# Third to seventh batch on the second batch's schedule of folds and transforms, in an attention and Fourier-mixing kernel on one core

## The chip, the core and the metric

The kernel runs on one core of a Trainium2 chip. The core has five engines that take their instructions from queues of their own: TensorE (PE in the profile, with PEld for its weight loads), VectorE (DVE), ScalarE (ACT), GpSimd (POOL) and SyncE (SP), which here issues the DMA transfers. The metric is the device time of one execution in microseconds (us); lower is better.

## What is computed

Eight batches of 576 tokens, 8 heads of 64 channels. The first half is attention in which each query keeps its 32 largest scores; the second half is a Fourier mix over tokens and channels followed by an MLP of width 2048. Cut from the reference:

```python
scores = scale * np.matmul(q, k.transpose(0, 1, 3, 2))
kth = np.partition(scores, -32, axis=-1)[..., -32:-31]
scores = np.where(scores >= kth, scores, -1e9)
attn = softmax(scores)                      # max subtracted, divided by the sum
x = heads_to_channels(np.matmul(attn, v))   # (8, 576, 512)
X = np.fft.fft(np.fft.fft(x, axis=1), axis=2)
u = x + np.real(X)
un = (u - mean(u)) / np.sqrt(var(u) + 1e-6)
out = u + np.maximum(un @ w_ch1, 0.0) @ w_ch2
```

## The kernel before

**Tiles and steps.** A tile is 128 query rows of one head. A pair of heads makes nine tiles, a batch 36, the whole 288. The main loop runs one step `i` for each tile. In step `i` DVE finds the last of tile `i`'s 32 largest scores and the first of tile `i+1`'s (MAX8 at L422, MATCH_REPLACE8 at L424: four and three of each per tile); PE makes the scores of tile `i+3` (L398, the tails of the keys L368; the fifth tile of a pair, which holds the last rows of both heads and has `e` None, L383); ACT copies them to SBUF (L401, L372, L390). `bounds(i)` on POOL (`nt`, L431) turns the maxima into two biases; in the next step ACT makes the mask (L445), POOL subtracts it (L448) and ACT takes the exponential (L456). From the second batch on (except the last pair of the second batch and of the eighth) ACT splits the result into halves of words (L469), SP writes them to DRAM and reads them back transposed (L482, L485, L503), and PE multiplies by `v` in `attend` (L561) once a chunk of a pair is there.

**After a batch's attention.** `end` is the batch's last tile. The tokens' transform uses symmetry: `fold_tails` and `fold_ops` add and subtract halves of the tokens and the channels. `fold_ops(b, par, eng)` gives four operations for one parity of the output tokens: `sd` (L716), `zw` (L675), then `both` (the first eight instructions into `fg`) and the last (`third(2)`: four more). Their buffers have two tags in turn: `sd` and `fg` share "fold_s", `zw` has "fold_d", so the second parity's `sd` can be written only once PE has read the first parity's `fg`. `dft_tokens(b, par)` is the matmul with `fg` (`yp`, L752) and ACT's copies into `y`. `dft_channels(b, t)` (`mp`, L809 and L813) makes the channels' transform of token tile `t`, `add_mixed` adds it to `x` on POOL (L836), `stats` takes mean and variance on DVE, and `channels_first` (`tpu`, L878) transposes the sum for the MLP.

**The MLP in units.** `mlp_units(b)` cuts a batch's MLP into about 67 units: `hidden` (`hp`, L963, four matmuls) and `back` (`cp`, L990, two matmuls with 512 columns; L1029 for the tails). The first chunk of every batch but the first one uses a seven-product form instead (`cv`, `cw`, `cz`, L1160) with weight pieces brought back by DMA (L906) and sums on POOL (L1105, L1132). An fp32 matmul has two records in the profile. The units are appended to one queue when a batch arrives.

**What sets the order.** Everything is written out at build time. `at(step, where, fn, cost)` puts an operation into a plan; each step runs the plan's places in a fixed order. On PE the order is: scores, transposes of inputs, `pe1` (token transforms), `pe2` (channel transforms), `pe` (`channels_first`), the tails of the scores; `attend` follows at the end of a step. On POOL: the subtraction of the mask for tile `i-1`, then `pool0` (the folds), then `bounds(i)`, then `pool` and `pool2`. Between PE's fixed operations `some(limit)` takes units from the queue until a step's planned length `step_us` is reached. At each arrival `level` picks that length so that the queue is empty at the next arrival, by the planner's own costs (1.75 for a `back` unit, 8 x columns / 1200 for a `hidden` one):

```python
steps = range(i, next((a for a in arrivals if a > i), i + PER_BATCH))
rest, lev = sum(u[0] for u in queue + waiting), 0.0
while lev < 6.4 and sum(max(0.0, lev - fixed_cost(s)) for s in steps) < rest:
    lev += 0.02
```

What is over at the last arrival, and the last batch's own units, is worked off after the last tile.

**The schedule of a batch.** `T0` is `end` + 2 for the first batch, + 3 for the second (`soon`), + 4 for the last and + 5 for the others. `ft` holds the steps of the two token transforms, `fc` the first of the three steps of the channel transforms; the arrival is `fc` + 4 for all batches but the first and the last. The lines that the change touches stand at the end of this loop (L1375 to L1430).

Of the kernel before, what the change touches and what calls it, by code (L numbers as in the profile page):

```python
# [73 lines left out]
def kernel(  # L74
# [9 lines left out]
    nc = tc.nc  # L84
# [560 lines left out]
    def fold_channels(eng, z, f, c, n):  # L645

        def tt(dst, out, src, up, down, op):
            eng.tensor_tensor(out=dst[..., out], in0=src[..., up], in1=src[..., down], op=op)

        if n == 0:  # L650
            eng.tensor_copy(out=c[..., 0:Q1 + 1:Q1], in_=z[..., 0:Q1 + 1:Q1])
            up, down = slice(1, Q1), slice(Q2 - 1, Q1, -1)
            tt(c, up, z, up, down, ALU.add)
            tt(c, slice(Q1 + 1, Q2), z, up, down, ALU.subtract)
        elif n == 1:
            up, down = slice(0, Q0), slice(Q1, Q0, -1)
            tt(f, slice(0, Q0), c, up, down, ALU.add)
            tt(f, slice(Q1, Q1 + Q0), c, up, down, ALU.subtract)
            up, down = slice(Q1 + 1, Q1 + Q0), slice(Q2 - 1, Q1 + Q0, -1)
            tt(f, slice(Q0 + 1, Q1), c, up, down, ALU.subtract)  # L660
            tt(f, slice(Q1 + Q0 + 1, Q2), c, up, down, ALU.add)
            eng.memset(f[..., Q0:Q0 + 1], 0.0)
            eng.tensor_copy(
                out=f[..., Q1 + Q0:Q1 + Q0 + 1], in_=c[..., Q1 + Q0:Q1 + Q0 + 1]
            )
        else:
            up, down = slice(Q2 + 1, Q3), slice(DM - 1, Q3, -1)
            tt(f, up, z, up, down, ALU.subtract)
            tt(f, slice(Q3, DM - 1), z, up, down, ALU.add)
            eng.tensor_copy(out=f[..., Q2:Q2 + 1], in_=z[..., Q2:Q2 + 1])  # L670
            eng.tensor_copy(out=f[..., DM - 1:DM], in_=z[..., Q3:Q3 + 1])

    def fold_halves(eng, s_, z):
        for cols, op in ((slice(0, Q2), ALU.add), (slice(Q2, DM), ALU.subtract)):
            eng.tensor_tensor(out=z[..., cols], in0=s_[..., 0:Q2], in1=s_[..., Q2:DM], op=op)  # L675

    def fold_tails(b, eng):


        f, got = ftail[0:TAIL], []  # L680

        def first():
            got.append(batp.tile([P, DM + Q2], F32, name=f"zt_{b}", tag="fold_s")[0:TAIL])
            fold_halves(eng, x_of[b][0:TAIL, 4, :], got[0][:, 0:DM])
            channels(0)

        def channels(n):
            fold_channels(eng, got[0][:, 0:DM], f[:, 0:DM], got[0][:, DM:DM + Q2], n)

        def second():  # L690
            channels(1)
            eng.tensor_copy(out=f[:, DM:DM + 1], in_=got[0][:, DM + Q0:DM + Q0 + 1])

        return [first, second, lambda: channels(2)]

    def fold_ops(b, par, eng, space="own"):

        x = x_of[b]  # L700

        if space == "hT":
            sp = batp.tile([P, NIT * CW[0]], F32, name=f"fsp_{b}", tag="hT")

        def buf(n, name, cols=DM):
            if space == "hT":
                return sp[:, 2 * DM * n:2 * DM * n + 2 * cols].rearrange("p (s c) -> p s c", s=2)
            pool, tag = (batp, ("fold_s", "fold_d")) if space == "own" else (attp, ("PT0", "PT1"))
            return pool.tile([P, 2, cols], F32, name=f"{name}_{b}_{par}", tag=tag[n % 2], bufs=1)

        got = folded[b, par] = []

        def first():
            got.append(buf(0, "sd"))
            op = ALU.add if par == 0 else ALU.subtract
            eng.tensor_tensor(out=got[0], in0=x[:, 0:2, :], in1=x[:, 2:4, :], op=op)  # L716

        def second():
            got.append(buf(1, "zw"))
            fold_halves(eng, got[0], got[1])  # L720

        def third(n):
            if n == 0:
                got.append(buf(2, "fg", DM + Q2))
            fold_channels(eng, got[1], got[2][:, :, 0:DM], got[2][:, :, DM:DM + Q2], n)

        def both():
            third(0)
            third(1)

        return [first, second, both, lambda: third(2)]

    def dft_tokens(b, par):
        for g2 in range(2):
            half_of_tokens(b, par, g2)
        return 4.3
# [96 lines left out]
    def add_mixed(b, t):  # L833
        rows, x = ROWS[t], x_of[b]
        us = us_of[b, t > 1 and t < 4][0:rows, CHUNKS[CHUNK_OF[t][0]].index(t), :]
        nc.gpsimd.tensor_tensor(out=x[0:rows, t, :], in0=x[0:rows, t, :], in1=us, op=ALU.add)  # L836

    def stats(b, t):
        rows, mvb = ROWS[t], mv[b % 2]
        st6 = small.tile([P, 6], F32, name=f"st6_{b}_{t}", tag="st6")  # L840
        nc.vector.bn_stats(out=st6[0:rows], in_=x_of[b][0:rows, t, :])
        nc.vector.bn_aggr(out=mvb[0:rows, t, :], in_=st6[0:rows])
# [454 lines left out]
    def at(step, where, fn, cost=0.0):  # L1297
        plan.setdefault((step, where), []).append(fn)
        costs[step] = costs.get(step, 0.0) + cost
# [75 lines left out]
    for b in range(B):  # L1375
        end = PER_BATCH * (b + 1) - 1
        last = b == B - 1
        first, soon = b == 0, b == 1
        T0 = end + (2 if first else 3 if soon else 4 if last else 5)
        if first:  # L1380

            for op in fold_tails(b, nc.gpsimd):
                at(T0 - 1, "pool", op)

            def folds(b=b):
                for par, space in ((0, "own"), (1, "hT")):
                    for op in fold_ops(b, par, nc.vector, space):
                        op()
            at(T0, "dve", folds)
            ft, fc = (T0 + 1, T0 + 1), T0 + 1  # L1390
        elif soon:

            for n, op in enumerate(fold_tails(b, nc.gpsimd)):
                at(T0 - 2 + n, "pool0", op)
            for par in range(2):
                def folds(par=par, b=b, T0=T0):
                    for n, op in enumerate(fold_ops(b, par, nc.gpsimd)):
                        at(T0 + 1 + 3 * par + min(n, 2), "pool0", op)
                at(T0, "begin", folds)
            ft, fc = (T0 + 4, T0 + 7), T0 + 8  # L1400
        elif not last:
            for n, op in enumerate(fold_tails(b, nc.gpsimd)):
                at(T0 - 2 + n, "pool0", op)
            for par in range(2):
                def folds(par=par, b=b, T0=T0):
                    for n, op in enumerate(fold_ops(b, par, nc.gpsimd)):
                        at(T0 + (6 if par else 1) + n, "pool0", op)
                at(T0, "begin", folds)
            ft, fc = (T0 + 5, T0 + 11), T0 + 12
        else:  # L1410
            for op in fold_tails(b, nc.gpsimd):
                at(T0 - 1, "pool0", op)

            def folds(b=b):
                for op in fold_ops(b, 0, nc.vector) + fold_ops(b, 1, nc.vector, "PT"):
                    op()
            at(T0, "dve", folds)

            at(T0 + 1, "pe1", lambda: one_unit() + one_unit() if len(queue) > 1 else 0.0)
            ft, fc = (T0 + 1, T0 + 3), T0 + 4  # L1420
        for par in range(2):
            at(ft[par], "pe1", lambda b=b, par=par: dft_tokens(b, par), 4.3)
        for n, t in enumerate((0, 1, 4, 2, 3)):
            quick = first or last
            s = fc + (0 if first else n // 3 if last else n // 2)
            at(s, "pe2", lambda b=b, t=t, q=quick: dft_channels(b, t, q), 1.75)
            if not quick:
                at(s, "pool2", lambda b=b, t=t: add_mixed(b, t))
                at(s + 1, "dve", lambda b=b, t=t: stats(b, t))
            at(s + (1 if quick else 2), "pe", lambda b=b, t=t: channels_first(b, t), 0.6)  # L1430
            if first and t == 4:
                at(s + 1, "pe", lambda: (queue.extend(waiting), waiting.clear()) and 0.0)
        at(s + 1, "begin" if quick else "dve", lambda b=b: rsqrt(b))
        arrivals.append(s + (1 if quick else 2))
        at(arrivals[-1], "units", lambda b=b: (queue if b else waiting).extend(mlp_units(b)))
# [36 lines left out]
    def one_unit():  # L1472
        c, fn, _ = queue.pop(0)
        fn()
        return c
# [175 lines left out]
```

## Time and profile before

| what | us |
|---|---|
| median of 3 runs (1879.72 to 1884.17) | 1882.73 |
| the profiled execution, own time | 1882.96 |
| its span, first to last instruction | 1881.2 |
| PE busy / DVE busy / ACT busy / POOL busy | 1713.1 / 1582.7 / 1295.7 / 911.3 |
| MAX8 on scores still being worked on (L422, 864 of them) | 626.5, 749 ns each |
| `sd` of a fold on POOL (L716, 12 of them) | 28.4, 2368 ns each |
| PE waiting at `sp_t` (L368) for ACT's copies L390, 16 times | 24.4 |

The page cuts the span into 40 slices of 47 us and gives each engine's busy share in tenths. A PE record's length is modelled, so PE can be busy in the view and still have room. A wait is put down to whoever released it. The tiles' top-k ends at 1684.5 us of the span; what follows is PE work of the last batch, with the seventh batch's left-over units ahead of it.

### The profile page before, as it was taken

How to read it: one execution, taken by the hardware profiler on the slowest of the kernel's cores; microseconds unless marked ns; L12 is line 12 of the kernel's file. 1: busy time of each engine (PE TensorE's matmuls, PEld its weight loads, DVE VectorE, ACT ScalarE, POOL GpSimd, SP SyncE). 2: the span in 40 equal slices, each digit the busy share in tenths (PEclk: the TensorE clock that was granted, in tenths of full speed). 3: DMA queues.
4: the chain of work that ended last, by engine and by line, in shares of the span. 5: the costliest groups of instructions: out<-in, count | busy, mean ns of one | idle time of the engine just before them, and what ended most of it. 6: DMA issues, size and time to landing. Idle time of an engine off the chain costs nothing.

```text
span 1881.2 us, 26922 instructions
## 1 busy us (share of the span) xinstructions
PE 1713.1 (91%) x8134; PEld 1086.5 (58%) x8134; DVE 1582.7 (84%) x3301; ACT 1295.7 (69%) x3104; POOL 911.3 (48%) x1278
## 2 busy tenths in 40 slices
PE   5567699889899998989999999999999999999999
PEld 3344364364466654666456665666556655666677
DVE  7999999798899999998899998999999999862110
ACT  6878658576788778777777677777787678652100
POOL 4768643455645356354544465355544465341012
PEclk8887899899899999999999999999999999999999
DMA  5333026651468755585455854685466756440132
GB/s 167 105 96 109 24 60 171 175 138 51 118 155 212 178 125 129 149 214 131 123 144 151 215 128 121 141 229 147 125 155 180 179 133 143 121 117 6 51 110 72
DMA packets 516576, 249.16 MB, mean 132 GB/s; under 512 B 398288, under 2 KB 506448, under 8 KB 516432
## 3 DMA queue, kind: packets, MB, share of 16 engines
q1 hardware_dynamic: 515664, 247.23, 50.7%
q8 instruction: 65, 1.06, 0.2%
q14 instruction: 79, 0.65, 0.1%
q10 hardware_dynamic: 768, 0.21, 0.0%
HBM read 93.63 MB, written 84.74 MB: 95 GB/s over the span
## 4 chain that ended last, share of the span: by engine, by line
PE 66%; ACT 10%; DVE 9%; POOL 7%; issue 3%; DMA 3%; SPq 2%; POOLq 0%; DVEq 0%; ACTq 0%
PE hp L963 24%; PE cp L990 8%; PE o L561 7%; PE sp L398 5%; DVE m L422 4%; PE cw L1160 4%; DVE wk L424 4%; PE yp L752 3%; PE cv L1160 3%; PE cp L1029 3%; POOL wk L448 2%; ACT wk L469 2%; ACT wk L445 2%; PE sp_t L368 2%; ACT S L456 1%
## 5 line engine op out<-in xcount | busy, mean ns | idle before, releaser
L448 POOL TENSOR_TENSOR wk<-S,wk 128x576 f32<-128x576 f32 x288 | 406.7, 1412 | 532.5 <-ACT wk L445 509.8
L422 DVE MAX8 m<-wk 128x8 f32<-128x576 f32 x864 | 626.5, 749 | 6.1
L963 PE MATMUL hp<-unT,w 128*128 128x256 f32 (+1 forms) x2048 | 535.3, 412 | 3.8 <-ACT hT L967 2.6
L963 PEld LDWEIGHTS hp<-unT,w 128*128 128x128 f32 x2048 | 379.4, 192 | 134.5 <-issue 33.4
L424 DVE MATCH_REPLACE8 wk<-m,wk 128x576 f32<-128x576 f32 x576 | 427.4, 742 | 0.0
L469 ACT COPY wk<-S 128x576 uint16<-128x576 uint16 x468 | 288.7, 666 | 0.0
L445 ACT ACTIVATE wk<-S,nt 128x576 f32<-128x576 f32 x288 | 222.5, 773 | 92.6 <-POOL nt L431 91.8
L422 DVE MAX8 m<-S 128x8 f32<-128x576 f32 x288 | 213.9, 743 | 45.1 <-ACT S L372 45.1
L990 PE MATMUL cp<-w,hT 128*128 128x512 f32 x512 | 244.0, 613 | 0.0
L561 PE MATMUL o<-PT,v 128*64 128x256 f32 (+3 forms) x1440 | 203.9, 427 | 21.8 <-DMA PT<-planes 9.9
L967 ACT ACTIVATE hT<-hp 128x320 f32<-128x320 f32 (+1 forms) x256 | 103.4, 408 | 160.2 <-PE hp L963 159.2
L424 DVE MATCH_REPLACE8 wk<-m,S 128x576 f32<-128x576 f32 x288 | 213.5, 741 | 0.0
L456 ACT ACTIVATE S<-wk,nt 128x576 f32<-128x576 f32 x234 | 182.4, 780 | 38.3 <-POOL wk L448 37.3
L398 PE MATMUL sp<-kT,qT 64*128 64x512 f32 (+1 forms) x528 | 181.5, 684 | 12.2 <-ACT means L1348 5.1
L561 PEld LDWEIGHTS o<-PT,v 128*64 128x64 f32 x1440 | 117.0, 157 | 105.7 <-issue 33.8
L401 ACT COPY S<-sp 128x512 f32<-128x512 f32 (+1 forms) x264 | 141.5, 586 | 29.5 <-PE sp L398 28.2
L990 PEld LDWEIGHTS cp<-w,hT 128*128 128x128 f32 x512 | 92.9, 194 | 107.8 <-issue 106.0
L1105 POOL TENSOR_TENSOR hT<-hT 128x512 f32<-128x512 f32 x64 | 81.3, 1274 | 105.1 <-ACT hT L967 91.2
L431 POOL TENSOR_TENSOR nt<-m,cc 128x2 f32<-128x2 f32 x288 | 59.2, 206 | 140.3 <-DVE m L422 139.3
L368 PE MATMUL sp_t<-kt,qT 128*128 128x128 f32 x320 | 70.5, 303 | 43.3 <-ACT S L390 24.4
L368 PEld LDWEIGHTS sp_t<-kt,qT 128*128 128x128 f32 x320 | 55.2, 195 | 92.3 <-ACT S L390 32.4
L1160 PE MATMUL cw<-w,hT 128*128 128x256 f32 x448 | 105.9, 383 | 0.5 <-issue 0.4
(160 smaller groups left out, 2133.1 us busy)
## 6 DMA issues: line engine op xcount, KB each, us to landing
planes<-wk SPq DMA_DIRECT2D x208, 288.0 KB, 2.7
w<-w_parts SPq DMA_DIRECT2D x82, 512.0 KB, 4.7
space<-in_moe_w_ch_dram SPq DMA_DIRECT2D x32, 512.0 KB, 3.7
nat<-in_q_dram SPq DMA_DIRECT2D x128, 64.0 KB, 2.4
v<-in_v_dram SPq DMA_DIRECT2D x64, 128.0 KB, 2.9
out_dram<-x SPq DMA_DIRECT2D x32, 256.0 KB, 2.6
nat<-in_k_dram SPq DMA_DIRECT2D x62, 128.0 KB, 2.9
planes<-wk SPq DMA_DIRECT2D x52, 144.0 KB, 2.7
```

Source lines behind the costliest of these rows:

```text
L368: nc.tensor.matmul(sp[:, 0:P], lhsT=qT[:, q_end - P:q_end], rhs=kt_t, start=True, stop=True)
L398: nc.tensor.matmul(sp[r], lhsT=qT[hd, q_cols], rhs=kT[hd, :], start=True, stop=True)
L422: ops.append(lambda src=src, m8=m8: nc.vector.max(out=m8, in_=src))
L424: ops.append(lambda src=src, m8=m8: nc.vector.match_replace(w, m8, src, NEG))
L445: nc.scalar.activation(out=w, in_=Ssb[i], func=AF.Relu, scale=-FAR, bias=Nt[i][:, 1:2])
L448: nc.gpsimd.tensor_tensor(out=w, in0=Ssb[i], in1=w, op=ALU.subtract)
L456: nc.scalar.activation(out=Ssb[i] if by_dma(i) else w, in_=w, func=AF.Exp, bias=Nt.pop(i)[:, 0:1], accum_out=den_t[pair % 3][:, c:c + 1],)
L469: nc.scalar.copy(out=words[:, half, :], in_=src[:, half, :])
L561: nc.tensor.matmul(o[D * e:D * (e + 1), c0:c1], lhsT=vv[:, c, e, :], rhs=pt[:, NF if c == NF else (NF + 1) * e + c, c0:c1], start=(c == 0) ...
L963: nc.tensor.matmul(hp[:, 0:w], lhsT=w1[:, dt, P * it:P * (it + 1)], rhs=unT[:, dt, 0:w], start=(dt == 0), stop=(dt == NDT - 1),)
L990: nc.tensor.matmul(cp, lhsT=hT[:, it, P * n:P * (n + 1)], rhs=w2[:, it, :], start=(it == 0), stop=(it == NIT - 1),)
L1160: nc.tensor.matmul(dst, lhsT=h()[a][:, kc, :], rhs=rhs_of(kc), start=start and kc == 0, stop=kc == NK - 1, skip_group_check=True,)
```

## The change

The third to seventh batch take the branch that only the second batch took. The branch that they had is removed. `T0` is not changed. For them this means, counted from `T0`:

| | before | after |
|---|---|---|
| `fold_tails` on POOL | -2, -1, 0 | -2, -1, 0 |
| `fold_ops` of parity 0 | 1, 2, 3, 4 | 1, 2, 3, 3 |
| `fold_ops` of parity 1 | 6, 7, 8, 9 | 4, 5, 6, 6 |
| `dft_tokens` of parity 0 and 1 | 5 and 11 | 4 and 7 |
| `dft_channels` | 12 to 14 | 8 to 10 |
| arrival of the units | 16 (`end` + 21) | 12 (`end` + 17) |

No operation is added or taken away; the order of the instructions on PE, ACT, DVE, POOL and SP differs from the second batch's MLP on, since `level` gives other step lengths.

```diff
-        elif soon:
+        elif not last:
 
             for n, op in enumerate(fold_tails(b, nc.gpsimd)):
                 at(T0 - 2 + n, "pool0", op)
...
                         at(T0 + 1 + 3 * par + min(n, 2), "pool0", op)
                 at(T0, "begin", folds)
             ft, fc = (T0 + 4, T0 + 7), T0 + 8
-        elif not last:
-            for n, op in enumerate(fold_tails(b, nc.gpsimd)):
-                at(T0 - 2 + n, "pool0", op)
-            for par in range(2):
-                def folds(par=par, b=b, T0=T0):
-                    for n, op in enumerate(fold_ops(b, par, nc.gpsimd)):
-                        at(T0 + (6 if par else 1) + n, "pool0", op)
-                at(T0, "begin", folds)
-            ft, fc = (T0 + 5, T0 + 11), T0 + 12
```

## The prediction

> **What bounds the kernel now.** I read the page's slices first, then the windows view cut where the batches' MLP work arrives, then the chain of waits in the tail, then the timeline around one batch's folds. "Step" is one turn of the main loop: one tile's top-k on VectorE (DVE), with everything the planner hangs on it.
>
> ```profile
> PE   5567699889899998989999999999999999999999
> DVE  7999999798899999998899998999999999862110
> ```
>
> TensorE (PE) is not full in the first half, is full afterwards, and for the last six slices works nearly alone: that is the MLP work which the planner could not place beside the tiles.
>
> ```profile
> 521.80:753.40 231.60, 214.76 (x1021) 132.50 (x1022) 221.72 (x459) 182.33 (x436) 115.61 (x169) 0.98 0.65 162
> 753.40:962.00 208.60, 197.65 (x953) 124.61 (x951) 190.64 (x397) 156.90 (x371) 104.72 (x155) 0.98 0.61 153
> 1583.00:1684.50 101.50, 99.99 (x472) 65.73 (x471) 86.16 (x179) 63.84 (x152) 40.91 (x61) 1.00 0.49 133
> 1684.50:1881.20 196.70, 192.41 (x875) 143.95 (x871) 28.87 (x72) 33.37 (x84) 32.22 (x52) 1.00 0.18 59
> ```
>
> The columns after the length are busy PE, weight load, DVE, ACT, POOL. The first row is steps 86 to 127, in which the second batch's MLP is worked off: 5.51 us a step, DVE busy 5.28 of it (221.72/42), so DVE sets the pace. In the second (36 steps, 5.79 each) and more so in the third row PE does. The fourth row is the tail after the last tile, all PE.
>
> ```profile
> 1759.47 34.45 PE hp L963 x128
> 1749.16 10.30 PE cp L990 x24
> ```
>
> The chain of the tail gives PE's true rates: 269 ns for a 320-column matmul, 429 ns for a 512-column one, where the groups' means are 432 and 594 ns in the same tail.
>
> **What the skill says.** "Perfetto Trace Analysis", section Identifying the Most-Contended Engine: a busy share of matmuls is no measure of headroom, as matmuls are pipelined. The rates just shown agree. So the free time of PE in the first row is more than 231.6 - 214.8 = 16.8 us. The same page, Sequencer Loop and Tensor Engine Instruction (MATMUL, LD_WEIGHTS): an engine instruction waits for its semaphores and its resources, and ScalarE (ACT), DVE and GpSimd (POOL) are strict FIFO. The trace agrees: POOL's small `nt` operation came out only after the blocked fold ahead of it (below).
>
> **The change, part by part.**
>
> 1. *Earlier arrival.* Batches 3 to 7 have T0 = end+5 before and after; `fc` goes from T0+12 to T0+8, so their units arrive at end+17 in place of end+21. The second batch arrives at end+15 either way and the eighth at end+10. So three periods change: the second batch's units get 38 steps for 42, batches 3 to 6 keep 36, the seventh gets 29 for 25. Following `level` with the planner's own costs, its level goes from 4.76 to 5.06 in the first of these, stays 5.36 to 5.4, and goes from 6.42 to 6.24 in the last. At the eighth batch's arrival 7 `back` units of the seventh are left before and none after. A unit is two k-blocks of 512 columns, two fp32 records each: 7 x 4 x 0.429 = 12.0 us leave the tail and have to fit into steps 86 to 123, the only stretch that becomes denser. There PE has 16.8 us of shown idle time, and the MLP groups' busy time of 133.7 us (hp 38.7 + 30.2, cp 30.5 + 7.5, cw 15.3, cv 11.5) is at true rates 128 x 0.269 + 128 x 0.217 + 64 x 0.429 + 112 x 0.216 + 32 x 0.21 = 120.6: some 13 us more, 30 in all. It fits by the sum, but not every step has room: with less spare time PE's lumps reach DVE more often. I take 3 us of lengthening: **-9.0** (bounds -12 and 0).
>
> 2. *Folds closer.* Per batch POOL's operations are the same ones; the last of each half (L648 x2, 1.41 us, and two copies) move one step earlier into one step, and half 1 starts at T0+4 instead of T0+6. Half 1's `sd` takes the buffer tag of half 0's `fg` ("fold_s"), so it must wait for `dft_tokens(b, 0)`, issued on PE in the same step T0+4. Before, it came a step later. The second batch already has this schedule, and this is its price on POOL and, in the last line, DVE:
>
> ```profile
> 476.29 1.41 POOL L648 TENSOR_TENSOR fg<-zw 128x254 f32<-128x254 f32 x2
> 478.99 1.41 POOL L448 TENSOR_TENSOR wk<-S,wk 128x576 f32<-128x576 f32 x1 [0.89 <-ACT wk L445]
> 481.85 2.37 POOL L716 TENSOR_TENSOR sd<-x 128x1024 f32<-128x1024 f32 x1 [1.46 <-PE yp L752]
> 484.18 0.19 POOL L431 TENSOR_TENSOR nt<-m,cc 128x2 f32<-128x2 f32 x1
> 486.52 0.76 DVE L422 MAX8 m<-S 128x8 f32<-128x576 f32 x1 [2.88 <-ACT S L372]
> ```
>
> `sd` waits 1.46 for the transform; `nt` stands behind it, the ACT mask (L445) behind `nt`, ACT's copies of scores behind the mask, and DVE stops 2.88 us. The waits of PE between 476 and 523.5 are these:
>
> ```profile
> PE sp L398 <- ACT S L372: 1.6, 1, 1.6
> PE yp L752 <- POOL fg L662: 1.6, 2, 0.8
> PE yp L752 <- POOL fg L648: 0.7, 1, 0.7
> ```
>
> In the later batches PE runs up to a step behind, which hides `yp` behind `fg` at half 0: in the fourth batch `fg` ended at 899.8 and `yp` began at 902.9, and both move about one step. At half 1, POOL needs after the first transform sd 2.4 + nt 0.2 + sub 1.4 + zw 2.55 + nt and sub 1.6 + the first eight of fg 3.6 = 11.7 us, against PE work of about 11.2 (attend 2.9, then units and scores of three steps): I take 1.0 us a batch of the 2.3 seen, **+5.0** for five (bounds 0 and 12). Of the `nt` chain I take 0.5 us a batch of PE's 1.6, as PE has attention and `cp` work queued meanwhile: **+2.5** (0 and 8).
>
> 3. *A bubble that goes.* Before, the last step of the transition fell on a tile with e None, whose `sp_t` waits for ACT's copies with no unit between. The view of waits in short stretches at the transitions shows for the third to seventh batch 2.1, 2.3, 2.3, 0.6 and 0.6 us, such as:
>
> ```profile
> PE sp_t L368 <- ACT S L390: 2.3, 1, 2.3
> ```
>
> After, that tile comes three steps behind the arrival, with units between: three quarters of 7.9, **-6.0** (bounds -8 and 0). Against it, steps T0+7 to T0+9 now have no units: I put **+2.0** for waits of `sp_t` and `mp` there (0 and 5).
>
> 4. *The end.* The 6 units of `cp` (10.30 us above) between the last batch's transform and its first `hp` are gone, and with them the cover for the DVE additions and ACT copies there: **+1.5** (0 and 3).
>
> SP issues the same transfers; the weight pieces (L906) move with their units and keep their lead, costed at nothing. If one lands late it is the 5.3 us that `cp` L1029 waited once at 845.3. In POOL and DVE no operation is added.
>
> Sum: -9.0 + 5.0 + 2.5 - 6.0 + 2.0 + 1.5 = -4.0. From the profiled execution's 1882.96 (span 1881.2) that is **1879**; the median shown, 1882.73, differs by 0.2.
>
> **The rivals.**
>
> *Folds cost more than the backlog saves (slower).* Place: POOL's queue at step T0+4 of five batches. PE lags there by up to a step of 5.4 us, and the same step holds `attend` as well, so `sd` may wait several us, `nt`, ACT and DVE with it. For: the second batch shows the whole chain, with 9.1 us of PE waits between 476 and 523.5. Against: there the unit queue was empty, so nothing covered it. At 3.6 us a batch (the waits of part 3's unfilled steps among them) and with half of the bubbles kept: -9 + 18 - 3 + 1.5 = +7.5, **1890.5**. It decides from about 2.3 us a batch, where -9 - 6 + 2 + 1.5 is used up.
>
> *All cover holds (faster).* PE's lag hides all of part 2: -9 - 6 + 2 + 1.5 = -11.5, **1871.5**. Against: 11.7 us against 11.2 leaves no margin.
>
> *The gain is hidden anyway (no change).* The first stretch lengthens by 8 instead of 3, as DVE then meets PE's lumps (it lost 2.9 us to one at 628): +1, **1884**. Against: a third of PE's work there is movable units.
>
> **How the numbers follow.** Chances: forecast 0.48 (own range 1873 to 1885), slower rival 0.32, full gain 0.10, no change 0.10. The range 1869 to 1892 takes in most of the first two and half of the third. With 0.2% (3.8 us) as what can be told from no change: faster 0.27 + 0.10 + 0.01 = 0.38; same 0.18 + 0.03 + 0.08 = 0.29; slower 0.03 + 0.29 + 0.01 = 0.33.
>
> **What would show it.** Part 1: the last tile ends about 6.5 us later (1684.5 + 3 of part 1 + 3.5 of parts 2 and 3), and the tail after it is some 10.5 us shorter than 196.7, at about 186. Part 2: five more waits of `sd` on `yp` of 1 to 3 us, and `yp` on `fg` at half 1 near 1 us each; over 2.3 us of PE idle per batch means the slower rival. Part 3: PE's waits of `sp_t` on S L390 fall from 24.4 us in all to under 18. A late `cp` L1029 or a longer time per step in batches 4 to 6 would make the forecast wrong.

## The result, and the profile after

The changed kernel takes 1901.59 us (median of 5 runs, 1895.61 to 1904.58) against 1882.99 for the kernel before: a ratio of 1.0091, 95% interval 1.0065 to 1.0116. It is slower by about 18 us, where the forecast had it faster by 4. The profiled execution took 1902.08 us, with a span of 1900.3 us.

The page's busy shares in 40 slices, after, for PE and DVE:

```profile
PE   5567699889899998989899999999899999999999
DVE  8999999798899989979799889989799898883110
```

The low tail of DVE is shorter by about a slice, as the change meant it to be, but DVE now shows a 7 in slices 18, 20 and 29, where the page before had none after slice 8. Slices 18 and 20 (808 to 855 and 903 to 950 us, at 47.5 us a slice) hold the two places shown below. The view of windows, cut at steps 86 to 123 (the denser stretch) and at the last tile's end, has after the length the busy time of PE, weight load, DVE, ACT and POOL, then the clock that was granted to TensorE (1 is full), the DMA share and GB/s:

```profile
523.90:743.80 219.90, 206.42 (x974) 130.24 (x975) 200.70 (x416) 168.34 (x402) 108.72 (x161) 0.97 0.64 156
1715.80:1900.30 184.50, 179.82 (x821) 132.36 (x817) 29.70 (x72) 30.64 (x78) 33.28 (x52) 1.00 0.18 61
```

The tail, the work after the last tile, is 184.5 us for 196.7: 12.2 us shorter. But the last tile ends at 1715.8 for 1684.5. Cut by steps (a step ends with its tile's last MAX8), the loss lies here:

| steps | before, us | after, us | difference |
|---|---|---|---|
| 1 to 85, the same program | 521.8 | 523.9 | +2.1 |
| 86 to 115 | 164.4 | 168.2 | +3.7 |
| 116 to 127 | 67.2 | 73.9 | +6.7 |
| 128 to 163 | 208.6 | 216.4 | +7.8 |
| 164 to 199 | 212.6 | 215.8 | +3.2 |
| 200 to 235 | 203.2 | 213.1 | +9.9 |
| 236 to 271 | 205.2 | 206.9 | +1.7 |
| 272 to 287 | 101.5 | 97.6 | -3.9 |
| tail | 196.7 | 184.5 | -12.2 |

PE's waits after, over the whole span (us in total, times, longest):

```profile
PE sp_t L368 <- ACT S L401: 27.0, 15, 6.8
PE sp_t L368 <- ACT S L390: 15.6, 9, 3.3
PE cp L1029 <- DMA w<-w_parts: 13.8, 6, 6.5
PE yp L752 <- POOL fg L648: 11.0, 6, 3.0
PE yp L752 <- POOL fg L662: 4.6, 6, 0.8
```

Before, the two rows of `sp_t` stood at 18.7 and 24.4 us. The other three, and the two rows of DVE that matter below, were these; the two of `yp` belonged to the second batch alone:

```profile
PE cp L1029 <- DMA w<-w_parts: 5.6, 2, 5.3
PE yp L752 <- POOL fg L662: 1.6, 2, 0.8
PE yp L752 <- POOL fg L648: 1.2, 2, 0.7
DVE m L422 <- ACT S L372: 45.1, 21, 6.3
DVE x L605 <- PE tpx L601: 45.5, 22, 5.8
```

After, DVE's two rows are:

```profile
DVE m L422 <- ACT S L372: 61.3, 16, 8.6
DVE x L605 <- PE tpx L601: 60.4, 26, 12.1
```

Together they grew by 31.1 us, and the tail shrank by 12.2. That leaves 18.9 us, and the two spans differ by 19.1. So the loss is time in which DVE waited.

Two places stand behind most of it, as the experiments below show. The first is a batch's fold. This is the timeline of the fourth batch's, from the rows of POOL, then one row each of PE, ACT and DVE (start, length, then the idle time before it and who ended it):

```profile
910.78 1.27 POOL L1019 TENSOR_TENSOR x<-x,hT 128x512 f32<-128x512 f32 x1 [3.80 <-ACT hT L1017]
911.99 0.20 POOL L651 COPY fg<-zw 128x4 f32<-128x4 f32 x1
912.13 1.41 POOL L648 TENSOR_TENSOR fg<-zw 128x254 f32<-128x254 f32 x2
916.91 0.20 POOL L431 TENSOR_TENSOR nt<-m,cc 128x2 f32<-128x2 f32 x1
...
914.01 0.46 PE L752 MATMUL yp<-fs,fg 128*64 128x145 f32 x2 [2.97 <-POOL fg L648]
...
917.14 0.78 ACT L445 ACTIVATE wk<-S,nt 128x576 f32<-128x576 f32 x1 [6.44 <-POOL nt L431]
...
925.54 0.76 DVE L422 MAX8 m<-S 128x8 f32<-128x576 f32 x1 [6.73 <-ACT S L372]
```

L1019 is the last addition of the *previous* batch's token tile 2. Its input comes from a `cp` unit that PE finished late. In POOL's queue it stands between the first half's `zw` and `fg`, so POOL waits 3.80 us for PE; the folds into `fg` wait behind it; PE comes to `yp` and waits 2.97 us for POOL; `nt` waits behind the folds, the mask on ACT 6.44 us behind `nt`, ACT's score copies behind the mask, and DVE stops for 6.73 us. (The tails of the scores that the last of these copies takes leave PE only after 923.7, behind the late `yp`, so PE and ACT both hold it up.) In the order of POOL's instructions L1019 has that place in batches 4 to 6; for the third it is one operation earlier, before `zw`. In all four, PE waits for `fg` in the first half. Before the change L1019 stood just ahead of, or among, the second half's folds, and PE waited for no `fg` of these batches. In the fourth batch, before:

```profile
922.60 1.27 POOL L1019 TENSOR_TENSOR x<-x,hT 128x512 f32<-128x512 f32 x1 [2.03 <-ACT hT L1017]
```

Here POOL waited too, 2.03 us, but PE came to the second half's `yp` late enough not to notice.

The second place is the end of the seven products. The timeline of SP, PE and DVE around 842 us:

```profile
833.62 2.38 SPq L503 DMA_TRANSPOSE PT<-planes  x1
836.76 1.17 SPq L906 DMA_DIRECT2D w<-w_parts  x2
...
830.52 3.72 PE L1160 MATMUL cw<-w,hT 128*128 128x256 f32 x16
...
841.97 3.68 PE L1029 MATMUL cp<-w,hT 128*64 128x512 f32 x6 [6.51 <-DMA w<-w_parts]
846.77 1.94 PE L1029 MATMUL cp<-w,hT 128*64 128x512 f32 x8
...
849.12 0.42 DVE L605 TENSOR_TENSOR x<-tpx,rd 128x256 f32<-128x256 f32 x1 [12.07 <-PE tpx L601]
```

The plain weights that the tails' units (L1029) need can be asked for only when the last product (`cw`) has read the combined ones, which by the view is at 834.2. SP's queue holds a transposing transfer and a write ahead of the request, so it goes out at 836.76, while PE comes to the units at once. PE waits 6.51 us, `tpx` stands behind it on PE, and DVE, whose next instruction reads `tpx`, stops for 12.07 us.

At both places PE's granted clock drops as well. The windows view has it (the column before the last two) at half in a stretch within or right behind each stop:

```profile
839.80:846.60 6.80, 4.63 (x11) 1.69 (x11) 0.00 (x0) 0.00 (x0) 0.00 (x0) 0.50 0.48 151
914.90:918.30 3.40, 3.02 (x22) 2.64 (x22) 3.33 (x8) 1.16 (x2) 2.51 (x9) 0.50 0.00 0
```

In the first of these, six records of `cp` L1029 took 3.68 us; from 846.77 on, eight took 1.94 with the clock back at full.

### The profile page after: what moved, and what is told of

The parts are those of the page before. It is cut to its first block, busy times and chain, and to the rows that moved or that the text cites. A ratio compares the mean times of both kernels' runs of the same rounds, so it can differ in the third digit from the quotient of the medians.

```text
span 1900.3 us, 26949 instructions
## 1 busy us (share of the span) xinstructions
PE 1710.7 (90%) x8134; PEld 1086.3 (57%) x8134; DVE 1584.2 (83%) x3301; ACT 1293.6 (68%) x3104; POOL 911.8 (48%) x1278
## 4 chain that ended last, share of the span: by engine, by line
PE 55%; DVE 11%; ACT 11%; POOL 11%; DMA 6%; issue 4%; SPq 2%; POOLq 0%; DVEq 0%; ACTq 0%
PE hp L963 21%; PE cp L990 7%; PE o L561 5%; DVE m L422 5%; DVE wk L424 5%; PE sp L398 4%; POOL wk L448 4%; PE cv L1160 3%; PE yp L752 3%; PE cp L1029 3%; PE cw L1160 3%; ACT wk L445 2%; DMA planes<-wk 2%; ACT wk L469 2%; DMA w<-w_parts 2%
## 5 line engine op out<-in xcount | busy, mean ns | idle before, releaser
L990 PE MATMUL cp<-w,hT 128*128 128x512 f32 x512 | 239.6, 603 | 0.0
L561 PE MATMUL o<-PT,v 128*64 128x256 f32 (+3 forms) x1440 | 199.0, 421 | 12.3 <-DMA PT<-planes 10.5
L398 PE MATMUL sp<-kT,qT 64*128 64x512 f32 (+1 forms) x528 | 169.4, 670 | 10.5 <-ACT means L1348 5.1
L401 ACT COPY S<-sp 128x512 f32<-128x512 f32 (+1 forms) x264 | 141.6, 587 | 38.4 <-PE sp L398 37.3
L990 PEld LDWEIGHTS cp<-w,hT 128*128 128x128 f32 x512 | 90.9, 191 | 94.3 <-issue 94.1
```

Of the source, the lines that this page charges most:

```text
L398: nc.tensor.matmul(sp[r], lhsT=qT[hd, q_cols], rhs=kT[hd, :], start=True, stop=True)
L401: nc.scalar.copy(out=s_t[r, keys], in_=sp[r])
L561: nc.tensor.matmul(o[D * e:D * (e + 1), c0:c1], lhsT=vv[:, c, e, :], rhs=pt[:, NF if c == NF else (NF + 1) * e + c, c0:c1], start=(c == 0) ...
L990: nc.tensor.matmul(cp, lhsT=hT[:, it, P * n:P * (n + 1)], rhs=w2[:, it, :], start=(it == 0), stop=(it == NIT - 1),)
```

## The experiments

Each was timed beside the kernel before on the same chip; that kernel's medians in the three groups were 1884.14 (e1 to e4), 1887.77 (e5 to e8) and 1884.26 (e9 to e12), so ratios are compared. Distances in us are ratio differences times 1884.

**e1: the addition of tile 2 on DVE.**

```diff
-                    elif t == 3:
+                    elif t == 3 or (t == 2 and 1 <= b < B - 2):
                         late_next.append(finish)
```

> The changed kernel, with the last addition of token tile 2 (L1019) of batches 2 to 6 moved from POOL to DVE, as tile 3's is: POOL no longer waits there for PE's last matmul of that tile. Theory Q (POOL's queue: that addition waits for PE, the next batch's fold waits behind it, PE waits for the fold, nt waits behind the fold): the waits of yp for fg fall from 12.8 us to under 5, and the time falls by 6 to 10 us, to about 1893. Theory W (weight pieces land late for cp L1029: 13.8 us waited against 5.6 before) and theory D (the 12 us of MLP work moved ahead of the last tile are simply not absorbed): no change, 1899 to 1904.

Measured: 1869.05 us, ratio 0.9922 (0.9905 to 0.9938), which is 32 us below the changed kernel. The fold of the fourth batch on POOL:

```profile
895.81 1.41 POOL L448 TENSOR_TENSOR wk<-S,wk 128x576 f32<-128x576 f32 x1 [0.89 <-ACT wk L445]
897.15 0.20 POOL L651 COPY fg<-zw 128x4 f32<-128x4 f32 x1
905.32 2.38 POOL L716 TENSOR_TENSOR sd<-x 128x1024 f32<-128x1024 f32 x1 [0.73 <-PE yp L752]
```

`fg` follows the mask's subtraction at once. Over the span `yp` waits for `fg` 2.8 us instead of 15.6, and DVE's row is

```profile
DVE m L422 <- ACT S L372: 31.5, 14, 6.0
```

29.8 us less than in the changed kernel. The place was right and the size was not: I had expected 6 to 10 us. The time fell by about as much as DVE's stops did. The granted clock also differs: 0.99 in steps 86 to 287, for 0.98 in the changed kernel.

**e2: the new folds, the old arrival.**

```diff
-        arrivals.append(s + (1 if quick else 2))
+        arrivals.append(s + (1 if quick else 2) + (4 if 1 < b < B - 1 else 0))
```

> The changed kernel's folds and transforms, but the units of batches 3 to 7 arrive 4 steps later, at end+21 as in the kernel before: the planner's levels and the work left for the tail are those of before. Theory Q: the folds stand as tight as in the changed kernel, so most of the loss stays, 1893 or more. Theory W: the units stand where they stood, so the weight pieces are late as seldom as before, about 1885. Theory D: the work is spread as before, 1880 to 1886.

Measured: 1865.22 us, ratio 0.9897 (0.9877 to 0.9917). All three expectations missed: with the old arrival the tight folds are 19 us faster than the kernel before. (By e9 and e10 below, 8.5 of these are the folds in themselves; the other 11 go with collisions of the same two kinds that the kernel before had and this one has not.) Here L1019 stands behind the second half's `fg` and PE's waits of `cp` L1029 for `w_parts` are 0.3 us in all in steps 86 to 287. So the folds' own chain, which the prediction charged with 7.5 us, is not what the change costs; what hurts is where the earlier units put other instructions.

**e3: nt ahead of the folds.**

```diff
-        run(i, "pool0")
         some_sums(max(2.1 - planned, 0.0))
         bounds(i)
+        run(i, "pool0")
```

> The changed kernel, with bounds(i) (nt) ahead of the folds in POOL's queue in every step. Theory Q in its second half (nt, the ACT mask and the score copies wait behind the blocked fold): DVE's waits for S L372 fall from 45.7 us to under 35 and the time by 3 to 8 us, to about 1896. If the first half (PE waits for fg) is all of it: no gain, as the folds now wait for DVE's maxima too, 1900 to 1908. Theories W and D: no change within 3 us.

Measured: 1876.16 us, ratio 0.9955 (0.9940 to 0.9970), 26 us below the changed kernel. PE still waits for `fg` (11.1 and 3.8 us), and DVE's row falls to

```profile
DVE m L422 <- ACT S L372: 44.4, 12, 8.8
```

That is far more than the 3 to 8 us expected. Steps 86 to 287 are 17.8 us shorter in its profile (1174.1 for 1191.9); another 8.2 us come in the first 85 steps (515.7 for 523.9), which hold the first two batches' folds and have nothing to do with the change. But not all of the 17.8 is the collision's: e11 below, with both collisions gone, has 12.4 us less than e7 in the same steps (1123.8 for 1136.2) by the same edit. So `nt` behind a fold costs with and without the collisions, and by that comparison only some 5 of the 17.8 us belong to the blocked fold.

**e4: without the transfers that restore the weights.**

```diff
-                if not last:
-                    bring(B21, second, part)
```

> The changed kernel without the two transfers that bring the plain weights back into one quarter of w_ch2 after each seven-product form (bring(B21)): that quarter keeps the last combined piece, so later products with it use other weights. cp L1029 then has no transfer to wait for. Theory W: the time falls by 8 us or more, to 1893 or less. Theories Q and D: within 3 us of the changed kernel, 1898 to 1904.

Measured: 1875.57 us, ratio 0.9956 (0.9940 to 0.9972), 25 us below the changed kernel, while `yp`'s waits (11.0 and 4.6) and DVE's for S L372 (62.4) stay. DVE's waits for `tpx` are 35.5 us instead of 60.4. So the late weights are a second loss, beside the first.

**e5: the tails' units ahead of the products.** Nothing is left out here; the units that need the plain weights run while these are still in place.

```diff
-                units.insert(1 - NIT, begin)
+                first_tails = not last
+                if first_tails:
+                    units += [
+                        (1.75, lambda ch=ch, p=p: back(ch, 4, p), "back") for p in range(4)
+                    ] + [(0.0, begin[1], "back")]
+                else:
+                    units.insert(1 - NIT, begin)
                 units += products
-            for t in [t for t in CHUNKS[ch] if t == 4 or not seven]:
+            for t in [t for t in CHUNKS[ch] if (t == 4 and last) or not seven]:
...
-            if b and not last:
-                need((b, 0, "x", 4))
```

> The changed kernel, with the four units of the last token rows (cp L1029) ahead of the seven products of the same chunk in place of behind them, so that no unit needs the weight quarter that bring(B21) has just asked for; nothing is left out. Theory W (the late quarter holds PE in the changed kernel): like the kernel without B21, 1872 to 1882, and DVE's waits for tpx fall from 52 to about 30 us. If leaving out B21 helped only by taking two transfers of 256 KB off the queue: no change, 1896 to 1904.

Measured: 1872.94 us, ratio 0.9937 (0.9911 to 0.9962), 29 us below the changed kernel. The row of `cp` L1029 waiting for `w_parts` is gone from PE's waits and DVE's for `tpx` is at 38.2 us. So it was the order, not the amount of traffic: every transfer is still made.

**e6 and e8: the controls on the kernel before** (the edits of e4 and of e1).

> The kernel before without bring(B21), a control (products after it use other weights, as in e4). If the lateness is what the change brought: the kernel before had 5.6 us of such waits and one DVE stop of 4 us, so it gains 3 to 6 us, to about 1879. If B21 costs every schedule the same: 20 us or more, to 1863 or less.

> The kernel before with the addition of tile 2 on DVE, the control of e1. Before, L1019 stands behind the second half's fg or between its zw and fg, where PE comes later. Theory Q (it is the place ahead of the first half's fg that costs): within 5 us of the kernel before, 1878 to 1886. If the addition on POOL costs any schedule: 20 us less or more.

Measured: e6 1878.98 us, ratio 0.9955 (0.9942 to 0.9968), a gain of 8.5 us; e8 1883.51 us, ratio 0.9979 (0.9964 to 0.9994), a gain of 4 us. The same edits gave 25 and 32 us in the changed kernel. e6 is somewhat over the 3 to 6 us expected; e8 is within its 5.

**e7 and e9: both mends, after and before.** e7 is the changed kernel with the edits of e1 and e5, e9 the kernel before with the same.

> The changed kernel with both mends, the addition on DVE (e1) and the tails first (e5). If the two losses stand at different places and both pace DVE, they add: 1901.6 - 32 - 24 gives about 1846 (1843 to 1855). If they are one loss seen twice: no better than e1, 1866 to 1871.

> The kernel before with both mends (addition of tile 2 on DVE, tails first): what the change is worth once its two collisions are out of the way is the distance from here to e7. The parts that the mends touch gave the kernel before 4 us (e8) and up to 9 (e6): 1874 to 1879. If the change itself is worth what the prediction put on it without parts 2 and the mends (-9 - 6 + 2 + 1.5 = -11.5), this run is at 1857; if the change brings more than that, it is above 1865.

Measured: e7 1845.84 us, ratio 0.9788 (0.9764 to 0.9812); e9 1872.79 us, ratio 0.9941 (0.9926 to 0.9956). The two mends take 57 us off the changed kernel where singly they took 32 and 29: they nearly add. DVE's two rows have 52.8 us less in e7 than in the changed kernel (29.9 and 39.0). e9 is slightly faster than the 1874 to 1879 expected. And the change itself, once neither collision is there, is worth 29 us by the ratios (27 by the medians), more than twice the 11.5 that the prediction gives without its part 2. In the profiles 12.7 of these are the tail (197.4 to 184.7) and 13.3 are in steps 86 to 287 (1149.5 to 1136.2).

**e10: both mends, the old arrival** (the edits of e7 and e2).

> Both mends and the changed kernel's folds, with the arrival 4 steps later (end+21) as in e2. If the early arrival is a gain in itself (12 us of work out of the tail), this is slower than e7 by 8 to 12 us, 1853 to 1858. If the early arrival is a loss in itself, as e2 against the changed kernel could be read, it is faster than e7, 1840 or less.

Measured: 1864.03 us, ratio 0.9896 (0.9879 to 0.9912). From e9 to e10, the folds alone, 8.5 us; from e10 to e7, the four steps of earlier arrival, 20 us by the ratios and 18 by the medians, of which 196.5 - 184.7 = 11.8 are the tail in the profiles. That is more than the 8 to 12 us expected. e10 also equals e2: with the late arrival there was nothing to mend.

**e11: both mends and nt first.**

> Both mends and nt ahead of the folds (e3). If nt behind a fold still holds ACT and DVE after the mends, another 8 us or more go, 1838 or less; the second batch's own fold chain (some 8 us of e3's gain stood in the first 85 steps) is in that. If the mends took the whole chain away: within 4 us of e7, 1842 to 1850.

Measured: 1826.51 us, ratio 0.9693 (0.9679 to 0.9708), the fastest of all, 58 us below the kernel before. Its waits of DVE for S L372:

```profile
DVE m L422 <- ACT S L372: 16.2, 7, 6.2
```

**e12: the changed kernel, arrival one step later** (as e2, with 1 in place of 4).

> The changed kernel, units of batches 3 to 7 arriving one step later (end+18). The last addition of tile 2 (L1019) then stands between zw and fg of the second half, as in no batch of the changed kernel. Theory Q (a collision of places): the half-0 chain is free, the time falls by 10 us or more, to 1891 or less. If the loss grows with the earliness of the arrival (theory D): a quarter of the way from the changed kernel to e2, 1891 to 1894.

Measured: 1894.19 us, ratio 1.0046 (1.0031 to 1.0060). That is what theory D allowed: by the ratios 8.5 us, about a quarter of the way to e2. Theory Q missed. The profile shows that the collision has moved, not gone. In batches 4 to 7 L1019 now stands ahead of the second half's `fg` (POOL, then PE), in the third ahead of the first half's:

```profile
916.79 1.27 POOL L1019 TENSOR_TENSOR x<-x,hT 128x512 f32<-128x512 f32 x1 [1.84 <-ACT hT L1017]
918.01 0.19 POOL L651 COPY fg<-zw 128x4 f32<-128x4 f32 x1
...
920.02 0.46 PE L752 MATMUL yp<-fs,fg 128*64 128x145 f32 x2 [1.47 <-POOL fg L648]
```

`yp`'s two waits are 12.0 and 4.0 us, close to the changed kernel's 11.0 and 4.6, and `cp` L1029 waits 18.4 us for `w_parts`, more than its 13.8. So this run alone does not tell theory D from a collision at another place. What does is e10 against e7: with the collisions gone, the earlier arrival is a gain of 18 to 20 us. The loss does not come from earliness as such, but from which instructions meet.

## Why the prediction was wrong, point by point

**The tail (part 1): right.** 12.0 us were to leave it and 1.5 to come back; it is 12.2 shorter, and `hp` waits for `unT` there 0.5 us. By PE's records what left is eight hidden units (`hp` 304 records for 368), not seven `back` units: the tail has 64 records of `cp` L990 before and after. At 0.217 us a record that is 13.9 us, so the size came out near all the same. Steps 86 to 115 are 3.7 us longer; the 3 taken was for steps 86 to 123, whose end already holds the third batch's folds. The arrival as such is a gain, larger than forecast (e10 to e7).

**The folds (part 2): this step failed.** The prediction said: "In the later batches PE runs up to a step behind, which hides `yp` behind `fg` at half 0". PE's being behind is just what made `fg` late: POOL had an instruction ahead of the fold that itself waited for PE. I had followed the instructions that the change moves, and the fold's own buffers, but not what else stands in POOL's queue between them; L1019 does not occur in the prediction. The wait came at half 0, not at half 1 where I had put it. It was also under-priced: 5.0 + 2.5 us were set against 32 (e1). The ground was "as PE has attention and `cp` work queued meanwhile", which asks only what PE loses. From 766 to 1512 us of the profile after, DVE was busy 669.4 us of 746.0, or 90%, so there was little room to make a stop of DVE good: its waits for S L372 fell by 29.8 us in e1 and the time by 32.

**The weight pieces: costed at nothing, measured at 29 us (e5).** "SP issues the same transfers" and they "keep their lead" was true of the products, none of which waits for its weights after the change, but the tails' units have no lead: they follow the product that frees the place. Whether other PE work falls between depends, by the plan, on where the units lie against the steps, which the change shifted; no run varied that alone. The single wait of 5.3 us at 845.3 before was the sign; I named it as the risk and priced it as one event for PE; it came six times, and the longest stopped DVE for 12 us.

**The bubble (part 3): named right, not gained.** `sp_t`'s waits for L390 fell from 24.4 to 15.6 us, below the 18 named. But its waits for L401 rose by 8.3, and `mp` waits 2.6 us more than before, where I had put 2.0 for both. The two rows of `sp_t` together went from 43.1 to 42.6, so the -6.0 is not to be seen in PE's waits. The new ones stand two steps behind the arrival, where the units were meant to cover them.

**The slower rival** had the right queue and the right direction, with `sd` as the waiting instruction. `sd` waits for `yp` only 6.9 us in all after step 85, and e2 and e10 show that this chain alone does not eat the gain: `sd` waits longer there, 9.1 us.

**The sum by measurement.** Mended, the change is worth -27 us (medians of e9 and e7). The two collisions cost the changed kernel 55.8 us (e7 to its 1901.6) and the kernel before 11.5 (e9): +44.3. Together that is +17. It closes by construction, as the same four medians give it, and shows only how the loss divides; that the loss is DVE's waiting rests on DVE's two rows and the tail (18.9 of 19.1 us).

What the runs leave open: which waits make up the mended change's 13.3 us inside the steps was not taken further. Nor was it separated how much of each mend goes through PE's clock. In steps 86 to 287 the windows view gives 0.98 for the kernel before, the changed kernel, e5 and e9, 0.99 for e1, e2 and e10, and 1.00 for e7 and e11. An estimate from these: one hundredth of 1192 us is 12 us of PE's time at full clock, not all of which need reach the end. A version before with the tails first alone, and one with `nt` first alone, were not tried.

## What to carry to other kernels

When a schedule moves, list for every in-order queue not only what the moved instructions wait for but what now stands ahead of them, and whether that waits for the very engine that they feed; such a loop stops both engines and everything queued behind. Price a stop at each engine that is nearly full, not only at the busiest: here DVE's stops of 6 to 12 us reached the end nearly whole. A schedule that turns out slower may be a good one with two chance meetings; take the meetings away before judging it, as e7 and e11 did.

## What the runs showed that I had not expected

Two mends of one queue place each, 32 and 29 us alone, made 57 together, so hardly any of the one was hidden by the other, although PE was busy for 94% of the time from 766 to 1512 us of the changed kernel's profile. And a small operation's place mattered as much as a large one's: `nt` takes 0.20 us, and putting it ahead of the folds was worth 26 us to the changed kernel and 18 to 19 us (e11 against e7) even with both collisions gone.
